# Clustered attention with an expert layer on one core: one-hot rows copied for two head pairs at once, and all five queues in another order

## The chip, the cores and the metric

The kernel runs on one core of a Trainium2 chip. The metric is the device time of one execution in microseconds. The five queues of a core are TensorE (PE), ScalarE (ACT), VectorE (DVE), GpSimd (POOL) and SyncE (SP, which issues DMA transfers).

## The reference

The input is q, k and v of 4 batches, 8 heads, 768 tokens and 64 elements, 16 centroids for each head, and two weight matrices. Each query and key is assigned to the centroid that it is most similar to. A query attends only to keys of its own cluster. The result, as 3072 rows of 512, passes through a layer of two matrix products with h times its softmax and a normalisation between them.

```python
q_assign = argmax(einsum('bhsd,hcd->bhsc', q_n, c_n)); k_assign = ...   # 16 clusters
mask = q_assign[..., :, None] == k_assign[..., None, :]
attn = softmax(where(mask, scale * q @ k.T, -1e9)); x = attn @ v          # (3072, 512)
h = x @ w_in; solu = h * softmax(h)                                       # (3072, 1024)
out = (solu - mean) / sqrt(var + 1e-6) * g_ln @ w_out
```

## The kernel before

**Masking by extra rows.** q and k of a pair of heads (p = 0 to 3 in each batch b) lie in the tiles `qbig` and `kbig`, features on the partitions. Under the 64 features stand one-hot rows of the cluster of each token, so that the product of scores adds a constant where the clusters agree. For batches 1 to 3 the rows 64 to 95 hold 32 rows: the one-hot rows of two heads, one from each of two neighbouring pairs (2d and 2d+1). The same 32 rows are copied into the tile of either pair, and of the odd pair's k the first 16 are set to zero afterwards (`blank`, named `bl`). There are six tiles each of `qbig` and `kbig`, used in turn (`slot`).

**Assignment.** Work comes in pieces: in batch 0 one pair with q and k together, in the other batches q (i = 0) or k (i = 1) of two pairs. A piece is loaded (`ld`, on SP), turned (`xt`, on DVE in batches 1 to 3; on PE with copies `xa` and `xt` in batch 0), cast into `qbig` and `kbig` (`ca`), multiplied with the centroids (`cl`, PE), turned back (`tb`), its maximum taken (`mx`), compared (`oh`), turned again (`ot`), all on DVE, and its one-hot rows are copied into place: `pl`, in `place` on line 458, one copy of 32 rows by 192 words for each pair, half of the tokens and head. v is loaded (`lv`) and cast (`cv`).

**Attention.** A unit n is two tiles of 128 queries of one or two heads. S n.k are its scores in three PSUM banks, E r the exponential of two banks on ACT (144 in all), V n.j the product with v, N g the normalisation of a group of units on DVE. The scores use two PSUM buffers, the exponentials five, the product with v one, so that the V of a group waits for the N of the group before.

**The layer.** For each f of 24 blocks of 128 tokens: `tx` turns x by DMA, `h` is the first product (two halves of two parts, two PSUM buffers), `hm` on DVE moves h out of PSUM with its maximum, `ex` on ACT is the exponential, `u` on DVE or POOL the product, `tu` turns u by DMA, `bn` and `ag` are statistics on DVE, `al` on POOL the factor, `y` the second product (four parts), `sc` on ACT or DVE moves y out of PSUM times the factor, `ou` stores it. `lo`, `li` load the weights, `wi` casts w_in, `su`, `ks`, `me` and `ce` centre w_out.

**The order.** `Plan.ORDER` (lines 23 to 175) lists every operation by name, written out for each of SP, PE, ACT, DVE and POOL. `Plan.run` issues each engine's operations in just that order; an operation may go to any of the engines that `add` allows, and the list it stands in decides. Waits come from the tiles that operations read and write. An engine runs its own list in order, so whatever stands behind a waiting operation waits too.

Of the kernel before, what the change touches and what calls it, by code (L numbers as in the profile page):

```python
# [18 lines left out]
class Plan:  # L19
# [5 lines left out]
            ld0.0.0 ld0.0.1 lg ld0.1.0.0 ld0.1.0 ld0.1.1.0 ld0.1.1 ld0.2.0.0 ld0.2.0  # L25
            ld0.2.1.0 ld0.2.1 lv0.0 ld0.3.0.0 ld0.3.0 ld0.3.1.0 ld0.3.1 lv0.1 lo1 lo0
            lv0.2 lo3 lo2 lv0.3 li0 li2 ld1.0.0.0 li3 li1 ld1.0.0.1 ld1.0.0.2 ld1.0.0
            tx0 ld1.0.1.0 ld1.0.1.1 ld1.0.1.2 ld1.0.1 ld1.1.0.0 ld1.1.0.1 ld1.1.0.2
            ld1.1.0 tx2 ld1.1.1.0 lv1.0 tu0 ld1.1.1.1 ld1.1.1.2 ld1.1.1 lv1.1 ld2.0.0.0
            ld2.0.0.1 ld2.0.0.2 tx4 tu1 ld2.0.0 ld2.0.1.0 tu2 ld2.0.1.1 ou0 ld2.0.1.2  # L30
            ld2.0.1 ld2.1.0.0 ld2.1.0.1 tu3 ld2.1.0.2 ld2.1.0 ou2 ou1 tu4 ld2.1.1.0
            ld2.1.1.1 ld2.1.1.2 ld2.1.1 lv1.2 ou3 ld3.0.0.0 lv1.3 tu5 ld3.0.0.1
            ld3.0.0.2 ld3.0.0 ld3.0.1.0 ld3.0.1.1 ld3.0.1.2 ld3.0.1 lv2.0 tx6 ld3.1.0.0
            ld3.1.0.1 ld3.1.0.2 ld3.1.0 tx8 tx10 lv2.1 ld3.1.1.0 tu6 lv2.2 ld3.1.1.1
            ld3.1.1.2 ou4 ou5 ld3.1.1 tu7 ou6 lv2.3 tu8 lv3.0 ou7 tu9 tu10 ou8 lv3.1
            tu11 lv3.2 ou9 tx12 lv3.3 tx14 ou10 tu12 ou11 tx16 tu13 tu14 ou12 ou13 tu15
# [64 lines left out]
            xa0.0.0 xa0.0.1 xt0.0.1 ca0.0.0.0 ca0.0.0.1 xa0.1.0 xt0.1.0 xa0.1.1 xt0.1.1
            xa0.2.0 xt0.2.0 ca0.1.1.0 xa0.2.1 xt0.2.1 E0 E1 E2 E3 xa0.3.1 E4 xt0.3.1 E5
            E6 E7 E8 E9 E10 E11 E12 E13 E14 ks E15 E16 E17 E18 E19 E20 E21 E22 E23 E24
            E25 E26 ex0 E27 E28 E29 E30 E31 E32 E33 E34 ex1 E35 E36 E37 E38 ex2 E39 sc0
            E40 E41 ca1.2.0 E42 ex3 E43 sc1 E44 ex4 E45 E46 sc2 E47 E48 ca1.2.1 E49 E50
            sc3 E51 ex5 E52 sc4 E53 E54 E55 E56 E57 E58 E59 E60 E61 E62 E63 E64 E65 E66
            sc5 E67 E68 E69 E70 E71 E72 E73 ca2.3.1 E74 E75 ex6 E76 E77 E78 ex7 E79 E80
            E81 E82 E83 ex8 E84 E85 sc6 E86 ex9 E87 sc7 E88 E89 E90 ex10 E91 E92 E93 E94
# [105 lines left out]
def kernel(  # L214
# [57 lines left out]
    def slot(b, p):  # L272
        return (b * n_pair + p) % R
# [784 lines left out]
```

## Time and profile before

| | |
|---|---|
| Median of three runs | 242.8 us (242.77 to 244.27) |
| Profiled execution | 243.15 us, span 241.3 us |
| Mean granted TensorE clock | 0.986 |
| Busy in the span | PE 90%, DVE 81%, ACT 80%, POOL 68% |
| First exponential E0 starts, last E143 ends | 15.57 us, 220.32 us |
| ACT's idle time between exponentials waiting for scores | 23.1 us, longest 4.6 us |
| One-hot copies on POOL, median | 0.34 us |
| One-hot copies on DVE, median and longest | 0.30 us, 1.55 us |

Times in a timeline are counted from the first instruction of the span. An idle time is put down to what ended it. Matmul ends are modelled in the profile, so a busy PE is not PE at its peak.

### The profile page before, as it was taken

The page shows a single profiled execution, that of the slowest core. Times are in us where ns is not written, and L with a number is a line of the kernel's source. Part 1 is how long each engine was busy: PE and PEld are TensorE (multiplying, and loading weights), DVE is VectorE, ACT ScalarE, POOL GpSimd, SP SyncE. Part 2 cuts the span into 40 slices and gives each one's busy share as a digit, 9 for nine tenths or more (in the row PEclk, how much of TensorE's full clock was granted, in tenths as well). Part 3 has the DMA queues.
Part 4 walks back from the last instruction along what each step waited for, and adds up shares of the span by engine and source line. Part 5 has one row for each costly group of instructions (what it writes and reads, how often), then busy time and mean ns, then how long its engine had stood idle before and what let it go on. Part 6 is the DMA issues. An engine that isn't in the chain of part 4 may idle for free.

```text
span 241.3 us, 6307 instructions
## 1 busy us (share of the span) xinstructions
PE 216.2 (90%) x2367; PEld 149.4 (62%) x2400; DVE 195.1 (81%) x432; ACT 193.4 (80%) x238; POOL 163.6 (68%) x275
## 2 busy tenths in 40 slices
PE   1999948798999886999999999999989999998983
PEld 1567625556766553777676767787767687675441
DVE  5399995989798994799799899878999676495992
ACT  2699845877998794999898979899988988897461
POOL 2898990079789987489947889889683512646751
PEclk9999997999999997999999999999999999999999
DMA  7999971899999999997969892857362325447522
GB/s 194 250 274 382 333 174 16 103 180 190 194 160 200 159 224 162 204 186 159 161 132 207 209 222 46 161 148 168 57 147 26 109 46 130 101 80 186 143 87 90
DMA packets 132159, 38.60 MB, mean 160 GB/s; under 512 B 123416, under 2 KB 127520, under 8 KB 132128
## 3 DMA queue, kind: packets, MB, share of 16 engines
q1 hardware_dynamic: 130560, 37.80, 75.3%
q10 hardware_dynamic: 1568, 0.39, 0.7%
q8 instruction: 19, 0.31, 0.6%
q14 instruction: 12, 0.10, 0.1%
HBM read 23.11 MB, written 6.29 MB: 122 GB/s over the span
## 4 chain that ended last, share of the span: by engine, by line
PE 59%; DMA 12%; ACT 10%; DVE 8%; POOL 6%; issue 4%; ACTq 0%; POOLq 0%; DVEq 0%
PE sps L551 18%; PE yps L706 12%; PE hps L638 11%; PE ops L568 10%; DMA xT<-x 8%; ACT e L556 5%; PE csc L428 4%; DMA uT<-u 4%; DVE kbig L408 2%; POOL u L667 2%; ACT xt L381 1%; DVE bs L678 1%; DVE x L591 1%; ACT y L712 1%; PE tp L373 1%
## 5 line engine op out<-in xcount | busy, mean ns | idle before, releaser
L556 ACT ACTIVATE e<-sps 128x1024 bf16<-128x1024 f32 x144 | 141.3, 1023 | 24.4 <-PE sps L551 23.1
L551 PE MATMUL sps<-qbig,kbig 80*128 80x256 bf16 (+4 forms) x648 | 96.4, 265 | 5.8 <-DVE kbig L408 4.3
L551 PEld LDWEIGHTS <-kbig 80*128 80x128 bf16 (+2 forms) x648 | 61.6, 121 | 32.0 <-issue 11.3
L568 PEld LDWEIGHTS <-e 128*128 128x128 bf16 x1152 | 54.4, 98 | 13.8 <-issue 1.6
L568 PE MATMUL ops<-v,e 128*128 128x65 bf16 x1152 | 59.4, 194 | 0.5 <-DVE x L591 0.3
L638 PE MATMUL hps<-w_in_sb,xT 128*128 128x512 bf16 x175 | 50.1, 379 | 4.3 <-DMA xT<-x 2.8
L706 PE MATMUL yps<-w_out_c,uT 128*128 128x512 bf16 x168 | 48.3, 386 | 4.2 <-DMA uT<-u 3.0
L667 POOL TENSOR_TENSOR u<-e_sb,hn 128x1024 bf16<-128x1024 bf16 x16 | 34.3, 2145 | 18.7 <-ACT e_sb L660 18.3
L678 DVE BATCH_NORM_STATS2 bs<-u 128x6 f32<-128x512 bf16 x48 | 32.1, 683 | 0.4 <-POOL u L667 0.2
L660 ACT ACTIVATE e_sb<-hn,hm 128x1024 bf16<-128x1024 f32 (+1 forms) x26 | 28.0, 1078 | 4.5 <-DVE hn L648 4.5
L406 POOL CAST qbig<-xt 64x1536 bf16<-64x1536 f32 (+1 forms) x15 | 19.7, 1312 | 12.5 <-DVE xt L398 11.9
L706 PEld LDWEIGHTS <-uT 128*128 128x128 bf16 x192 | 17.5, 99 | 15.4 <-DMA uT<-u 3.3
L638 PEld LDWEIGHTS <-xT 128*128 128x128 bf16 x192 | 16.8, 97 | 13.1 <-DMA xT<-x 3.3
L648 DVE TENSOR_SCALAR_CACHE_REDUCE hn<-hps 128x512 f32<-128x512 f32 x24 | 16.2, 676 | 8.1 <-PE hps L638 7.3
L458 POOL COPY qbig<-oht 32x192 f32<-32x192 f32 x47 | 18.1, 387 | 6.6 <-DVE oht L448 4.5
L398 DVE STREAM_TRANSPOSE xt<-raw 128x768 f32<-128x768 f32 x24 | 22.2, 951 | 0.2 <-DMA raw<-in_k_dram 0.2
L648 DVE TENSOR_SCALAR_CACHE_REDUCE hn<-hps,hm 128x512 f32<-128x512 f32 x24 | 17.7, 737 | 4.4 <-PE hps L638 4.0
L591 DVE TENSOR_TENSOR x<-ops,den 128x256 bf16<-128x256 f32 (+1 forms) x40 | 19.1, 477 | 1.4
L694 POOL TENSOR_TENSOR esq<-esq,mv 128x1 f32<-128x1 f32 x24 | 5.9, 246 | 20.7 <-DVE mv L682 19.5
L408 POOL TENSOR_SCALAR kbig<-xt 64x1536 bf16<-64x1536 f32 (+1 forms) x14 | 17.6, 1255 | 1.0
L458 POOL COPY kbig<-oht 32x192 f32<-32x192 f32 x46 | 16.3, 356 | 2.2
L696 POOL TENSOR_TENSOR alpha<-esq,halves 128x1 f32<-128x1 f32 x24 | 14.7, 612 | 1.9
(91 smaller groups left out, 220.1 us busy)
## 6 DMA issues: line engine op xcount, KB each, us to landing
vf<-in_v_dram SPq DMA_DIRECT2D x16, 384.0 KB, 4.4
out_dram<-y SPq DMA_DIRECT2D x24, 256.0 KB, 3.1
raw<-in_q_dram SPq DMA_DIRECT2D x31, 192.0 KB, 4.3
raw<-in_k_dram SPq DMA_DIRECT2D x31, 192.0 KB, 4.1
w_g<-in_moe_w_out_dram SPq DMA_DIRECT2D x4, 512.0 KB, 7.1
w_st<-in_moe_w_in_dram SPq DMA_DIRECT2D x4, 512.0 KB, 10.6
uT<-u SPq DMA_TRANSPOSE x22, 3.3
xT<-x SPq DMA_TRANSPOSE x14, 3.6
```

The lines of the kernel that those rows point to most:

```text
L398: nc.vector.transpose(xts[b, d, i][:, hh], raws[b, d, i][:, hh])
L408: eng.tensor_scalar(dst, src, scalar1=inv_C, scalar2=1.0, op0=Alu.mult, op1=Alu.mult)
L458: (nc.vector if e == "DVE" else nc.gpsimd).tensor_copy(dst, src)
L551: nc.tensor.matmul(sps_[r][:, half, c0:c0 + w], kbig[z][u, h % 2, keys], qbig[z][u, h % 2, q0:q0 + w])
L556: nc.scalar.activation(es[r][:], sps_[r][:], Act.Exp, scale=exp_scale, bias=-exp_scale)
L568: nc.tensor.matmul(opss[g][:, s, :VW], es[r][:, half, c0:c0 + P], v1[slot(b, h // 2)][:, h % 2, kt, :VW], start=(kt == 0), stop=(kt == n_t ...
L638: nc.tensor.matmul(ff[f, "h", f2][:], xTs[f // 2][:, f % 2, dc, :], w_in_sb[:, dc, f2 * FF2:(f2 + 1) * FF2], start=(dc == 0), stop=(dc == ...
L648: nc.vector.tensor_scalar(ff[f, "hn"][:, f2, :], ff[f, "h", f2][:], scalar1=-1.0, scalar2=hm[:, 0:1] if f2 else None, op0=Alu.mult, op1=Al ...
L660: nc.scalar.activation(ff[f, "e"][:, r, :], ff[f, "hn"][:, r, :], Act.Exp, scale=-1.0, bias=ff[f, "hm"][:, 1:2], accum_out=ff[f, "esum"][: ...
L667: (nc.vector if e == "DVE" else nc.gpsimd).tensor_tensor(ff[f, "u"][:, r, :], ff[f, "e"][:, r, :], ff[f, "hn"][:, r, :], op=Alu.mult)
L678: nc.vector.bn_stats(ff[f, "bs"][:, f2, :], ff[f, "u"][:, f2, :])
L706: nc.tensor.matmul(ff[f, "y"][:], ff[f, "uT"][:, fc, :], w_out_c[:, fc, :], start=(fc == 0), stop=(fc == n_fc - 1))
```

## The change

The six tiles of q become three tiles that hold two pairs each, and so do those of k; `qbig` and `kbig` are now views of them. In batches 1 to 3 a piece's one-hot rows are copied by four operations `pd` (one for each head and half of the tokens) in place of eight `pl`: each writes the rows into both pairs, reading its source twice. The waits of scores and of `blank` name `pd` accordingly. In batch 0 nothing of this changes. There are 48 operations fewer.

All five lists are written anew. The number of operations on each engine goes from 147, 713, 210, 327 and 207 (SP, PE, ACT, DVE, POOL) to 147, 713, 207, 326 and 163. Of the operations that stay, 24 go from POOL to DVE, 20 from DVE to POOL, 10 from ACT to DVE, 7 from POOL to ACT, 2 from DVE to ACT and 2 from ACT to POOL. 76 `pl` leave POOL and 20 leave DVE; 41 `pd` come to POOL and 7 to DVE.

```diff
     R = 6
-    qbig = [big.tile([P, 2, S], BF16, name=f"qbig{i}") for i in range(R)]
-    kbig = [big.tile([P, 2, S], BF16, name=f"kbig{i}") for i in range(R)]
+    both = [[big.tile([P, 2, 2, S], BF16, name=f"{n}big{i}") for i in range(R // 2)] for n in "qk"]
+    qbig, kbig = ([t[:, pp] for t in ts for pp in range(2)] for ts in both)
...
+    def place_both(b, d, i, c, e):
+
+        hh, hf = divmod(c, 2)
+        (nc.vector if e == "DVE" else nc.gpsimd).tensor_copy(
+            both[i][slot(b, 2 * d) // 2][D:D + NB, :, hh, hf * HALF:(hf + 1) * HALF].bitcast(F32),
+            asg[(b, d, i), "oht"][c * NB:(c + 1) * NB, :].bitcast(F32).unsqueeze(1)
+            .to_broadcast([NB, 2, HALF // 2]))
...
-        return [f"pl{t[0]}.{2 * t[1] + pp}.{t[2]}.{hf}.{hh}" for pp in range(2) for hh in range(2)
-                for hf in range(2)]
+        return [f"pd{tag[j]}.{c}" for c in range(4)]
...
+            if by_token(b):
+                add(nm, "DVE POOL", (lambda e, x=x: place(*x, e)), [f"ot{n}"] + behind(x[0], x[1], "S"))
+            else:
+                add(nm, "DVE POOL", (lambda e, x=x: place_both(*x, e)),
+                    [f"ot{n}"] + behind(b, 2 * x[1], "S") + behind(b, 2 * x[1] + 1, "S"))
...
-            nd += [f"pl{b}.{p}.{t}.{hf}.{hh}" for t in range(2) for hf in range(2)]
+            nd += [f"pl{b}.{p}.{t}.{hf}.{hh}" if by_token(b) else f"pd{b}.{p // 2}.{t}.{2 * hh + hf}"
+                   for t in range(2) for hf in range(2)]
```

Of the lists, the parts that matter here. SP, from the weights on:

```diff
-            lv0.2 lo3 lo2 lv0.3 li0 li2 ld1.0.0.0 li3 li1 ld1.0.0.1 ld1.0.0.2 ld1.0.0
-            tx0 ld1.0.1.0 ld1.0.1.1 ld1.0.1.2 ld1.0.1 ld1.1.0.0 ld1.1.0.1 ld1.1.0.2
...
-            ld2.0.1 ld2.1.0.0 ld2.1.0.1 tu3 ld2.1.0.2 ld2.1.0 ou2 ou1 tu4 ld2.1.1.0
+            lo0 lo1 ld1.0.0.0 ld1.0.0.1 lo2 ld1.0.0.2 ld1.0.0 li2 lv0.3 ld1.0.1.0 li0
+            li3 ld1.0.1.1 ld1.0.1.2 li1 tx0 ld1.0.1 lv1.0 ld1.1.0.0 ld1.1.0.1 tx2
...
+            ld2.0.1.2 tu3 ld2.0.1 ou1 ld2.1.0.0 ld2.1.0.1 ou2 ld2.1.0.2 ld2.1.0 tu4
```

PE, where h0 and y4 stand:

```diff
-            S15.1 S15.2 S16.0 V14.0 V14.1 S16.1 V15.0 V15.1 S16.2 h0.0.0 h0.0.1 h0.1.0
-            S17.0 h0.1.1 S17.1 S17.2 cl1.0.0 h1.0.0 S18.0 S18.1 V16.0 h1.0.1 S18.2 V16.1
...
-            y3.2 y3.3 V31.1 S34.0 S34.1 V32.0 V32.1 y4.0 S34.2 y4.1 S35.0 y4.2 y4.3
+            S15.1 S15.2 S16.0 S16.1 V14.0 V14.1 S16.2 V15.0 S17.0 V15.1 S17.1 S17.2
+            cl1.0.0 S18.0 V16.0 S18.1 V16.1 S18.2 h0.0.0 h0.0.1 S19.0 h0.1.0 h0.1.1
...
+            S33.2 y3.2 y3.3 V31.1 S34.0 S34.1 V32.0 V32.1 S34.2 S35.0 y4.0 y4.1 S35.1
+            S35.2 V33.0 y4.2 S36.0 S36.1 y4.3 V33.1 S36.2 S37.0 V34.0 V34.1 V35.0
```

DVE, its first 50 operations or so:

```diff
-            xt0.0.0 gk tb0.0 mx0.0 oh0.0 ot0.0 pl0.0.1.1.1 pl0.0.1.1.0 pl0.0.0.0.0 bl0.0
-            pl0.0.0.0.1 tb0.1 mx0.1 oh0.1 ot0.1 pl0.1.0.1.0 xa0.3.0 tb0.2 pl0.1.1.0.1
-            xt0.3.0 mx0.2 pl0.1.1.1.1 oh0.2 N0 pl0.1.0.0.1 ot0.2 pl0.2.1.1.1 tb0.3 mx0.3
-            N1 pl0.2.1.0.1 pl0.2.1.1.0 oh0.3 pl0.2.0.1.1 ot0.3 N2 ca0.3.1.0 ca0.3.0.0
-            pl0.3.0.1.0 pl0.3.1.1.0 pl0.3.0.0.0 N3 ca0.3.0.1 ca0.3.1.1 N4 ce0 ce1 ce2 N5
-            ce3 ce4 ce5 N6 ce6 ce7 xt1.0.0.0 xt1.0.0.1 hm0.0 N7 hm0.1 tb1.0.0 mx1.0.0
+            xa0.0.1 xt0.0.0 ca0.0.0.0 gk xa0.1.0 tb0.0 mx0.0 oh0.0 ot0.0 pl0.0.1.1.1
+            tb0.1 pl0.0.1.0.0 mx0.1 pl0.0.0.0.0 bl0.0 ca0.1.0.0 xt0.2.1 oh0.1 ot0.1
+            tb0.2 pl0.1.0.1.0 mx0.2 oh0.2 cv0.0.1 pl0.1.1.0.1 pl0.1.1.1.0 pl0.1.0.0.0
+            xt0.3.0 ot0.2 cv0.1.1 pl0.1.0.1.1 N0 xt0.3.1 pl0.2.1.1.1 ca0.2.0.0
+            pl0.2.0.1.0 N1 tb0.3 mx0.3 pl0.2.0.1.1 oh0.3 ot0.3 N2 pl0.3.1.1.0 cv0.2.0
+            cv0.2.1 pl0.3.0.0.0 N3 pl0.3.0.1.1 pl0.3.1.0.1 ca0.3.0.1 xt1.0.0.0 N4
+            xt1.0.0.1 cv0.3.0 ce0 ce1 N5 ce2 ce3 ce4 N6 ce5 ce6 ce7 N7 wi1 tb1.0.0
+            mx1.0.0 oh1.0.0 ot1.0.0 hm0.0 hm0.1 N8 xt1.0.1.0 xt1.0.1.1 hm1.0 hm1.1 N9
```

POOL, at the end of batch 0:

```diff
-            ca0.2.1.1 cv0.2.0 pl0.3.1.0.0 pl0.3.1.0.1 pl0.3.1.1.1 bl0.3 pl0.3.0.1.1
-            cv0.2.1 pl0.3.0.0.1 wi0 cv0.3.0 cv0.3.1 wi2 wi3 wi1 ca1.0.0 ca1.1.0 u0
+            pl0.2.0.0.1 ca0.3.1.1 ca0.3.1.0 bl0.2 ca0.3.0.0 pl0.3.1.1.1 pl0.3.1.0.0
+            pl0.3.0.0.1 pl0.3.0.1.0 bl0.3 cv0.3.1 ca1.0.0 wi3 wi2 wi0 pd1.0.0.0 ca1.1.0
```

The other rows of the lists differ in the same manner: the operations are the same, save for those that are named above, and stand a few places earlier or later. ACT has E28 before `ex0` in place of E26, and `sc4`, `sc7`, `sc11`, `sc13` and `sc16` have gone from it to DVE, `sc22` has come.

More of the change, by code (lines that the diff above doesn't have):

```diff
@@ L97 @@
-            ptx23 h22.1.1 y19.0 y19.1 y19.2 y19.3 h23.0.0 h23.0.1 h23.1.0 y20.0 y20.1
-            y20.2 y20.3 h23.1.1 ptu22.0 y21.0 y21.1 y21.2 y21.3 ptu22.1 ptu23.0 y22.0
-            y22.1 y22.2 ptu23.1 y22.3 y23.0 y23.1 y23.2 y23.3""",
-        ACT="""
[L101 to L108, printed above, removed]
-            E95 ex11 E96 E97 E98 E99 E100 E101 E102 E103 E104 E105 E106 sc11 E107 E108
-            E109 E110 ex12 E111 E112 E113 ex13 E114 E115 E116 ex14 E117 E118 E119 sc12
-            E120 E121 ex15 E122 sc13 E123 E124 ex16 E125 E126 E127 E128 E129 E130 E131
-            E132 E133 E134 ex17 E135 E136 ex18 E137 E138 sc16 E139 ex19 E140 E141 ex20
-            sc17 E142 E143 ex21 sc18 ex22.0 sc19 ex22.1 sc20 tu22.0 ex23.0 ex23.1 sc21
-            tu23.0 sc23""",
@@ new lines @@
+            V8.1 S11.0 V9.0 V9.1 S11.1 S11.2 me S12.0 S12.1 S12.2 S13.0 V10.0 V10.1
+            V11.0 V11.1 S13.1 S13.2 S14.0 S14.1 V12.0 S14.2 S15.0 V12.1 V13.0 V13.1
+            S15.1 S15.2 S16.0 S16.1 V14.0 V14.1 S16.2 V15.0 S17.0 V15.1 S17.1 S17.2
+            cl1.0.0 S18.0 V16.0 S18.1 V16.1 S18.2 h0.0.0 h0.0.1 S19.0 h0.1.0 h0.1.1
+            V17.0 V17.1 h1.0.0 h1.0.1 S19.1 S19.2 S20.0 h1.1.0 V18.0 h1.1.1 S20.1 V18.1
+            S20.2 S21.0 V19.0 V19.1 S21.1 S21.2 cl1.0.1 S22.0 V20.0 S22.1 h2.0.0 S22.2
@@ new lines @@
+        ACT="""
+            xa0.0.0 xt0.0.1 ca0.0.1.0 xt0.1.0 ca0.0.1.1 xa0.1.1 xt0.1.1 ca0.0.0.1
+            ca0.1.0.1 xa0.2.0 xt0.2.0 xa0.2.1 ca0.1.1.0 E0 E1 E2 E3 xa0.3.0 E4 E5
+            xa0.3.1 E6 E7 E8 E9 ca0.2.1.0 E10 E11 E12 E13 E14 E15 ks E16 E17 E18 E19 E20
+            E21 E22 E23 E24 E25 E26 E27 E28 ex0 E29 E30 E31 E32 ex1 E33 E34 E35 ca1.1.1
+            E36 E37 sc0 ex2 E38 E39 E40 E41 ex3 E42 ca1.3.0 E43 E44 sc1 ex4 E45 E46 sc2
+            E47 ca2.1.0 E48 ca1.2.1 E49 E50 sc3 E51 E52 E53 ex5 E54 E55 E56 E57 E58 E59
+            E60 E61 E62 E63 E64 E65 E66 sc5 E67 E68 E69 E70 E71 E72 E73 E74 E75 E76 ex6
+            E77 E78 E79 E80 ex7 E81 E82 E83 E84 sc6 E85 ex8 E86 E87 ex9 E88 E89 E90 ex10
+            E91 E92 E93 E94 E95 ex11 E96 E97 E98 E99 E100 E101 E102 E103 E104 E105 E106
+            E107 E108 E109 ex12 E110 E111 E112 E113 E114 ex13 E115 E116 ex14 E117 ex15
+            E118 sc12 E119 E120 ex16 E121 E122 E123 E124 E125 E126 E127 E128 E129 E130
+            E131 E132 E133 E134 ex17 E135 E136 E137 ex18 E138 ex19 E139 E140 ex20 E141
+            sc17 E142 E143 ex21 sc18 sc19 ex22.0 ex22.1 sc20 tu22.0 ex23.0 ex23.1 sc21
+            tu23.0 sc22 sc23""",
@@ new lines @@
+        POOL="""
+            z1 z3 cb z5 z2 ca0.1.1.1 pl0.0.0.1.1 pl0.0.1.0.1 pl0.0.0.1.0 pl0.0.1.1.0 sg
+            pl0.0.0.0.1 cv0.0.0 z4 pl0.1.1.1.1 pl0.1.1.0.0 bl0.1 ca0.2.0.1 pl0.1.0.0.1
+            cv0.1.0 pl0.2.1.1.0 pl0.2.1.0.1 ca0.2.1.1 pl0.2.0.0.0 pl0.2.1.0.0
+            pl0.2.0.0.1 ca0.3.1.1 ca0.3.1.0 bl0.2 ca0.3.0.0 pl0.3.1.1.1 pl0.3.1.0.0
+            pl0.3.0.0.1 pl0.3.0.1.0 bl0.3 cv0.3.1 ca1.0.0 wi3 wi2 wi0 pd1.0.0.0 ca1.1.0
+            pd1.0.0.3 u0 pd1.0.0.1 ca1.0.1 pd1.0.0.2 pd1.0.1.0 al0 cv1.0.1 cv1.0.0
+            pd1.0.1.2 u1 pd1.0.1.3 u2 ca1.2.0 bl1.1 u3 al1 al2 cv1.1.0 ca1.3.1 u4
+            ca2.0.0 pd1.1.0.1 pd1.1.0.2 pd1.1.1.1 al3 pd1.1.1.3 cv1.1.1 pd1.1.1.0
+            pd1.1.1.2 al4 pd1.1.0.3 cv1.2.1 pd2.0.0.3 u5 ca2.2.0 ca2.0.1 pd2.0.0.0 bl1.3
+            ca2.1.1 al5 cv1.3.0 pd2.0.0.1 ca2.3.0 pd2.0.1.1 pd2.0.1.2 ca3.0.0 pd2.0.1.0
+            pd2.0.1.3 bl2.1 pd2.1.0.2 ca2.2.1 pd2.1.0.0 pd2.1.0.3 pd2.0.0.2 ca2.3.1
+            pd2.1.1.2 pd2.1.1.1 pd2.1.0.1 u6 pd2.1.1.3 cv2.1.1 pd2.1.1.0 u7 ca3.1.0 al6
+            cv2.2.0 al7 u8 bl2.3 u9 u10 al8 cv2.2.1 pd3.0.1.1 cv2.3.0 cv2.3.1 pd3.0.1.2
+            al9 pd3.0.0.2 pd3.0.1.0 bl3.1 al10 cv3.0.1 pd3.0.0.3 ca3.0.1 al11 pd3.1.0.1
+            cv3.2.0 pd3.1.1.1 cv3.0.0 pd3.1.1.2 u12 pd3.1.0.2 pd3.1.0.0 ca3.2.1 ca3.2.0
+            u13 pd3.1.0.3 al12 cv3.1.1 al13 u16 bl3.3 ca3.3.0 al14 al15 cv3.3.1 u17 al16
+            u18 u19 al17 u20 al18 u21 al19 al20 al21 al22 al23""",
@@ L855 @@
             x = tuple(map(int, nm[2:].split(".")))
-            add(nm, "DVE POOL", (lambda e, x=x: place(*x, e)), [f"ot{n}"] + behind(x[0], x[1], "S"))
+            if by_token(b):
[3 more added lines that the diff above has]
+                    [f"ot{n}"] + behind(b, 2 * x[1], "S") + behind(b, 2 * x[1] + 1, "S"))
     for b, p in pairs:
@@ L862 @@
             add(f"bl{b}.{p}", "DVE POOL", (lambda e, b=b, p=p: blank(b, p, e)),
-                [f"pl{b}.{p}.1.{hf}.{hh}" for hf in range(2) for hh in range(2)])
+                [f"pd{b}.{p // 2}.1.{c}" for c in range(4)])
     def make_c_b2():
```

206 lines of the change are left out of this document (87 added, 119 removed).

## The prediction

> **What bounds the kernel now.** First the page: busy time by engine.
>
> ```profile
> span 241.3 us, 6307 instructions
> PE 216.2 (90%) x2367; PEld 149.4 (62%) x2400; DVE 195.1 (81%) x432; ACT 193.4 (80%) x238; POOL 163.6 (68%) x275
> ```
>
> TensorE (PE) is the nearest to full, ScalarE (ACT) and VectorE (DVE) follow, GpSimd (POOL) has the most room. So the average names no bound; the table by stage does.
>
> ```profile
> 33.00:37.40 4.40, 0.47 (x5) 0.42 (x6) 4.33 (x3) 0.00 (x0) 3.46 (x5) 1.00 0.48 76
> 37.40:42.00 4.60, 4.60 (x41) 2.98 (x39) 2.26 (x5) 3.30 (x4) 0.00 (x0) 0.63 0.00 0
> ```
> ```profile
> 16.00:31.00 15.00, 14.67 (x192) 10.08 (x192) 14.24 (x34) 14.32 (x17) 13.14 (x27) 1.00 1.06 357
> ...
> 70.00:93.00 23.00, 19.30 (x191) 12.35 (x194) 21.65 (x47) 19.05 (x23) 20.90 (x32) 0.98 1.02 183
> 93.00:125.00 32.00, 31.72 (x375) 22.76 (x379) 24.77 (x53) 28.26 (x31) 22.75 (x39) 0.96 0.97 165
> 125.00:141.00 16.00, 15.50 (x174) 10.93 (x174) 14.71 (x33) 14.46 (x19) 13.19 (x19) 1.00 0.91 208
> 141.00:175.00 34.00, 33.43 (x387) 24.96 (x391) 28.99 (x67) 30.80 (x35) 28.50 (x47) 1.00 0.61 130
> ```
>
> The columns are length, then busy time of PE, PEld, DVE, ACT, POOL, then clock and DMA. From 93 to 175 us PE is busy 97 to 99% of the time: there it sets the pace. At 33 to 37.4 us PE and ACT stand still while DVE is busy. The list of waits and the timelines say why.
>
> ```profile
> ACT e L556 <- PE sps L551: 23.1, 29, 4.6
> ```
> ```profile
> 30.86 0.56 DVE L406 CAST qbig<-xt 64x768 bf16<-64x768 f32 x1
> 31.34 5.54 DVE L408 TENSOR_SCALAR kbig<-xt 64x768 bf16<-64x768 f32 x1
> ```
> ```profile
> 31.57 1.03 POOL L492 CAST w_in_sb<-w_st 128x1024 bf16<-128x1024 f32 x1
> 32.56 0.95 POOL L473 CAST v<-vf 128x384 bf16<-128x384 f32 x2
> 33.46 3.00 POOL L492 CAST w_in_sb<-w_st 128x1024 bf16<-128x1024 f32 x3
> ```
>
> The cast `ca0.3.1.1` takes 5.54 us; its like took 0.62 at 27.72. It ends when POOL's run of six casts ends (36.46), and these follow one another without a gap, each starting 0.05 us before its forerunner ends. The scores of head 7 wait for it, and E16 behind them: ACT idle 4.61 us. A second loss lies around 90 us:
>
> ```profile
> 94.93 1.02 ACT L556 ACTIVATE e<-sps 128x1024 bf16<-128x1024 f32 x1 [3.38 <-PE sps L551]
> ```
> ```profile
> 42.62 1.35 SPq L604 DMA_TRANSPOSE xT<-x  x1
> ...
> 87.27 1.29 SPq L672 DMA_TRANSPOSE uT<-u  x1
> ```
>
> S34.2 stands behind y4.0 on PE, which waits for uT of f=4 to land at 92.05. Its u ended at 81.61, but SP issued its turn at 87.27: SP issues back to back from tx0 at 42.62 on, after 7.77 us in which it only waited to issue tx0.
>
> **The change part by part.** *The copies.* 96 copies of 32x192 become 48 of 32x384.
>
> ```profile
> L458 POOL COPY qbig<-oht x47: 333/340/1073, 13.7 to 187.6; 32x192 f32<-32x192 f32 x47
> L458 DVE COPY qbig<-oht x17: 184/300/1553, 13.8 to 178.6; 32x192 f32<-32x192 f32 x17
> ```
>
> Columns: min/median/max ns. On POOL 76 go and 41 come, on DVE 20 go and 7 come. The trace has no 32x384 copy. On POOL its bounds are one old copy (0.34) and two (0.68); the nearest row is the cast of 128x384 to v, 0.50, which I take: 76 x 0.34 = 25.8 becomes 41 x 0.50 = 20.5, so -5.3 us, bounds -11.9 to +2.1. On DVE the bounds are 0.25 and 0.60 (one copy, two); I take 0.35, as v's cast there: 20 x 0.30 = 6.0 becomes 2.5, so -3.5, bounds -4.3 to -1.8. POOL's part is worth nothing in the sum: PE's matmuls cover it from 93 us on; without that cover it would be its 5.3 us.
>
> *Operations that change engine.* POOL to DVE 24, DVE to POOL 20, ACT to DVE 10, POOL or DVE to ACT 9. With the rows' medians and the copies above POOL's whole queue falls from 156 to 148.5 us, DVE's grows from 194 to 197.5, ACT's stays at 188. DVE grows because four more evictions of y (0.75 each), v casts, `wi1` and three early copies come to it.
>
> *The stall at 31 us goes.* `ca0.3.1.1` moves to POOL, ahead of `bl0.2`. DVE keeps one such cast, `ca0.3.0.1`, but POOL's neighbours are then `bl0.3` (0.41) and `cv0.3.1` (0.50); behind these POOL stands at `ca1.0.0`, which waits for `xt1.0.0.1`, two transposes behind the cast on DVE. So the long run of casts can't meet it: -4.6. With PE not idle for 4 us I expect the clock of 0.63 at 37.4 to 42 to rise, and E18's wait of 1.28 behind the mean matmul (1.71) to fall to some 0.8: -0.5.
>
> *DVE's queue in batch 0.* Ahead of N3 sixteen operations come (four copies of x by 0.55, three casts by 0.66, four v casts by 0.35, five one-hot copies) and ten go: 6.5 against 3.2, so +3.3. `xa0.0.1`, `ca0.0.0.0` and `xa0.1.0`, together 1.7, fit into DVE's idle 1.32 and 1.89 before tb0.0 at 10.45. That leaves +1.6; four more operations that can meet POOL, at some 0.15 each, make it +2.2 (bounds 0 and 3.9). Queued behind are N0 to N3, for which V2, V4, V6 and V8 wait.
>
> *h0 and the weights.* SP now issues three loads of piece 1.0.1 (1.55, 0.73, 1.36) before tx0, in the time in which it waited; PE runs S17 and S18 before h0. E25's wait of 2.08 goes. But `wi1` now stands on DVE before tb1.0.0 and hm0 (0.65 by the 64x768 casts of 0.56 to 0.63; at most POOL's 1.03), and h0 comes later, so ex0 will wait for hm0; from E28's place to hm0's I reckon 1.8. Together -0.3, bounds -2.1 to +2.
>
> *y4.* SP's lead is those 3.6 us and what N5, for which tx0 waits, comes earlier. S34.2 and S35.0 pass y4.0. Up to 3.4 is to be had (u of f=4 goes from DVE to POOL, 1.21 to 2.14, which the 5.7 us that its turn stood in SP's queue cover). What is late next is DVE, 94% busy from 70 to 93: between N8 and N14 it gets 2.3 more (two transposes of the next batch, one oh and ot, less u4). So -1.1, bounds -3.4 to +2.3.
>
> *From 97 us on.* I summed the matmuls that stand ahead of each E on PE: the two orders differ by 1.4 us at most. A lead is carried to the end, nothing is added. The four evictions on DVE cost 3.0 there, hidden by PE, since DVE is 77 and 85% busy at 93 to 125 and 141 to 175; without this cover they cost 3.0 and their waits (2.8 us over six rows of L714, so 1.9 over four).
>
> The sum: -4.6 - 0.5 + 2.2 - 0.3 - 1.1 = -4.3 us. The profiled execution took 243.15 (span 241.3), 0.35 above the median of 242.8; 243.15 - 4.3 gives 238.9.
>
> **The rivals.** *The lead is larger.* If DVE's 2.3 us between N8 and N14 are covered and ex0 waits for nothing, the terms are -5.1 + 2.2 - 2.1 - 3.4 = -8.4: 234.8. For it: SP is late with every turn from 65 to 92 us (u3 ended at 77.66, its turn went at 82.54). Against: 94% on DVE.
>
> *The stall moves.* `cv0.3.0` on DVE stands directly behind `xt1.0.0.1`, the operation that also frees POOL's `ca1.0.0`, behind which `wi3 wi2 wi0` are ready. If POOL starts first and runs without a gap, DVE waits 1.46 + 3 x 1.03 less the overlaps = 4.4, and V10, ce0 and N5 with it: 243.3. For it: the six casts at 31 us. Against: DVE starts its next operation some 0.08 before the last ends, POOL began `ca1.0.0` 0.06 after.
> The Trainium skill ("SBUF — State Buffer", "Who interferes with whom") says that whichever of the two issues first holds the shared pair for its whole instruction; read as one instruction, DVE would wait 1.46 us at most and the time would be 240.4 by that estimate. The trace disagrees with that reading: at 31.34 DVE waited through six.
>
> *Hidden anyway.* ACT's chain of exponentials and PE from 93 us on take back all that was won before, say all but 1 us: 242.1. For it: the 97 to 99%. Against: PE's work ahead of each E is unchanged, so there is nothing to take it back.
>
> *Slower: DVE becomes the bound.* If DVE's queue has no usable idle time between N0 and N33, its tally decides: ahead of N33 it has 6.6 us more than before, the stall of 4.9 is off it, and the four evictions wait 1.9: 243.15 + 6.6 - 4.9 + 1.9 = 246.7. It decides from the point where DVE's share passes PE's in the windows from 50 us on. For it: 95% at 16 to 31 and 94% at 70 to 93. Against: 77% after 93.
>
> That the joined copy doesn't do what it says, and costs two old ones, adds 2.1 on POOL, hidden: no other time.
>
> **How the numbers follow.** Forecast 42%, with a range of its own of 236.8 to 240.8; larger lead 12%, stall moved 12%, hidden 10%, slower 24%. About 1% (2.4 us) is what a measurement of this kernel can tell from no change. Faster by more: the larger lead and nearly all of the forecast, 0.52. Within: the stall moved, hidden, and the forecast's upper edge, 0.24. Slower: 0.24. The range goes from 235.0 to 246.5, which cuts the outer halves of the two end cases.
>
> **What would show it.** Right: E16 at 33 to 35 us instead of 37.42, no ACT wait over 2 us before 60, tx0 issued near 39, the turn of f=4 before 83, E54 4 to 5 us before its 97.63, POOL's copies at 0.45 to 0.55. Wrong: a DVE cast of over 2 us beside POOL casts (`cv0.3.0` first of all), N3 after 34, DVE busier than PE from 141 to 175, or a lead at 97 us that is gone at 200.

## The result and the profile after

The changed kernel takes 233.15 us (median of 4 runs, 231.92 to 234.03) against 243.54 of the kernel before beside it: ratio 0.956, 95% interval 0.949 to 0.963, so 10 us less. Run a second time, with four runs more, it took 232.22, ratio 0.959 [0.954, 0.964]. The forecast of 238.9 lies above, and so does the lower end of its range, 235.0. Of the rivals the larger lead, 234.8, came nearest.

The page of the profiled execution (231.92 us):

```profile
span 229.9 us, 6272 instructions
PE 213.6 (93%) x2368; PEld 148.0 (64%) x2400; DVE 189.8 (83%) x431; ACT 193.6 (84%) x235; POOL 152.0 (66%) x231
```

Nearly the same work of PE now fills 93% of a shorter span. The stages (length, PE, PEld, DVE, ACT, POOL, clock, DMA share, GB/s):

```profile
31.00:43.00 12.00, 10.84 (x153) 7.84 (x154) 11.20 (x25) 10.84 (x13) 5.87 (x9) 1.00 0.84 226
70.00:93.00 23.00, 22.59 (x240) 15.08 (x242) 20.37 (x44) 22.72 (x26) 20.46 (x30) 1.00 1.09 200
93.00:125.00 32.00, 31.72 (x393) 23.57 (x398) 28.23 (x61) 28.79 (x33) 26.53 (x34) 1.00 0.88 171
125.00:141.00 16.00, 15.78 (x167) 10.84 (x169) 14.32 (x33) 14.41 (x19) 11.06 (x14) 1.00 0.78 174
141.00:175.00 34.00, 33.10 (x371) 24.79 (x376) 28.08 (x61) 29.80 (x36) 24.64 (x37) 1.00 0.53 127
```

From 70 to 93 us PE was busy 19.30 of 23 us and is now busy 22.59, while DVE fell from 21.65 to 20.37. From 93 us on PE's shares are much what they were. ACT's waits for scores, in all, times, longest:

```profile
ACT e L551 <- PE sps L546: 14.2, 34, 1.1
```

They were 23.1 in all and 4.6 at the longest. The stall of 31 us is gone: on POOL's timeline `ca0.3.1.1` is the first of these two casts (0.83 us each), and on DVE's the cast `cv0.3.0` behind the transpose, where one rival saw the stall move to, takes 0.32.

```profile
26.18 1.73 POOL L398 TENSOR_SCALAR kbig<-xt 64x768 bf16<-64x768 f32 x2
```
```profile
36.23 0.97 DVE L388 STREAM_TRANSPOSE xt<-raw 128x768 f32<-128x768 f32 x1
37.12 0.32 DVE L468 CAST v<-vf 128x384 bf16<-128x384 f32 x1
```

The turn of f=4 goes at 81.11 in place of 87.27, and PE stands 0.24 us ahead of y4.0 where it stood 2.69. SP's queue after:

```profile
36.92 4.25 SPq L484 DMA_DIRECT2D w_st<-in_moe_w_in_dram  x1
41.27 1.66 SPq L599 DMA_TRANSPOSE xT<-x  x1
...
81.11 2.29 SPq L667 DMA_TRANSPOSE uT<-u  x1
```

PE at y4.0, before and after (in brackets the idle time ahead of it and what ended it):

```profile
92.09 0.61 PE L706 MATMUL yps<-w_out_c,uT 128*128 128x512 bf16 x1 [2.69 <-DMA uT<-u]
```
```profile
85.44 1.04 PE L701 MATMUL yps<-w_out_c,uT 128*128 128x512 bf16 x3 [0.24 <-DMA uT<-u]
```

SP issues the load `li1` straight ahead of tx0 at 41.27; the 7.77 us in which it only waited are filled. The joint copies (min/median/max ns):

```profile
L450 POOL COPY qbig<-oht x21: 496/500/722, 48.3 to 169.7; 32x384 f32<-32x384 f32 x21
L450 DVE COPY kbig<-oht x4: 352/368/1442, 57.9 to 166.1; 32x384 f32<-32x384 f32 x4
```

Where the 11.4 us between the two spans were won, by the starts of the same exponentials (ACT's list has `ex0` and `ex5` in other places, so rows beside these are not taken):

| from, to | before | after | won |
|---|---|---|---|
| start to E12 | 27.54 | 30.08 | -2.5 |
| E12 to E20 (the stall) | 15.01 | 9.21 | 5.8 |
| E20 to E51 | 46.86 | 45.71 | 1.2 |
| E51 to E54 (y4) | 8.22 | 4.06 | 4.2 |
| E54 to E143 | 121.67 | 120.53 | 1.1 |
| E143 to the end | 22.00 | 20.31 | 1.7 |

The table is of one execution of either kernel. The experiments show which of its rows hold for others: not all of the 4.2 at y4 does.

### The profile page after: what moved, and what is told of

The parts are those of the page before. It is cut to its first block, busy times and chain, and to the rows that moved or that the text cites. A ratio compares the mean times of both kernels' runs of the same rounds, so it can differ in the third digit from the quotient of the medians.

```text
span 229.9 us, 6272 instructions
## 1 busy us (share of the span) xinstructions
PE 213.6 (93%) x2368; PEld 148.0 (64%) x2400; DVE 189.8 (83%) x431; ACT 193.6 (84%) x235; POOL 152.0 (66%) x231
## 4 chain that ended last, share of the span: by engine, by line
PE 69%; DVE 13%; ACT 7%; issue 4%; POOL 3%; DMA 3%; ACTq 0%; POOLq 0%; DVEq 0%
PE sps L546 21%; PE hps L633 15%; PE yps L701 14%; PE ops L563 12%; ACT e L551 5%; PE csc L418 4%; DMA uT<-u 2%; DVE qbig L445 1%; DVE mx L428 1%; PE tp L363 1%; ACT y L707 1%; DVE oht L438 1%; DVE oh L432 1%; DVE cst L424 1%; DVE xt L373 1%
## 5 line engine op out<-in xcount | busy, mean ns | idle before, releaser
L546 PE MATMUL sps<-qbig,kbig 80*128 80x256 bf16 (+4 forms) x648 | 94.1, 262 | 2.0 <-ACT e L551 1.1
L563 PEld LDWEIGHTS <-e 128*128 128x128 bf16 x1152 | 52.4, 97 | 13.5 <-DVE x L586 1.5
L563 PE MATMUL ops<-v,e 128*128 128x65 bf16 x1152 | 57.2, 193 | 1.1 <-DVE x L586 1.0
L662 POOL TENSOR_TENSOR u<-e_sb,hn 128x1024 bf16<-128x1024 bf16 x19 | 40.7, 2144 | 25.0 <-ACT e_sb L655 19.0
L701 PE MATMUL yps<-w_out_c,uT 128*128 128x512 bf16 x166 | 46.3, 379 | 2.0 <-ACT y L707 0.5
L701 PEld LDWEIGHTS <-uT 128*128 128x128 bf16 x192 | 17.4, 97 | 12.6 <-issue 1.3
L398 POOL TENSOR_SCALAR kbig<-xt 64x1536 bf16<-64x1536 f32 (+1 forms) x12 | 15.2, 1270 | 5.2 <-ACT xt L371 4.3
L396 POOL CAST qbig<-xt 64x1536 bf16<-64x1536 f32 (+1 forms) x12 | 16.3, 1355 | 0.7 <-DVE den L575 0.4
L575 DVE RECIPROCAL den<-ops 128x4 f32<-128x4 f32 (+1 forms) x40 | 7.1, 178 | 10.8 <-PE ops L563 10.7
L450 POOL COPY qbig<-oht 32x384 f32<-32x384 f32 x21 | 10.7, 510 | 6.4 <-DVE oht L438 4.4
L707 ACT ACTIVATE y<-yps,alpha 128x512 f32<-128x512 f32 x13 | 8.9, 686 | 6.8 <-POOL esq L687 2.6
```

Of the source, the lines that this page charges most:

```text
L396: eng.tensor_copy(dst, src)
L546: nc.tensor.matmul(sps_[r][:, half, c0:c0 + w], kbig[z][u, h % 2, keys], qbig[z][u, h % 2, q0:q0 + w])
L563: nc.tensor.matmul(opss[g][:, s, :VW], es[r][:, half, c0:c0 + P], v1[slot(b, h // 2)][:, h % 2, kt, :VW], start=(kt == 0), stop=(kt == n_t ...
L662: (nc.vector if e == "DVE" else nc.gpsimd).tensor_tensor(ff[f, "u"][:, r, :], ff[f, "e"][:, r, :], ff[f, "hn"][:, r, :], op=Alu.mult)
L701: nc.tensor.matmul(ff[f, "y"][:], ff[f, "uT"][:, fc, :], w_out_c[:, fc, :], start=(fc == 0), stop=(fc == n_fc - 1))
```

## The experiments

Ratios are to runs of the kernel before beside them on the same chip, with the 95% interval; 0.01 is 2.4 us. Profiled executions are single ones: one can lie 2 us or more beside its kernel's median, which is said where it matters.

**The order alone: `after_single`.** All lists of the changed kernel, with the old tiles and each joint copy written as its two old ones.

```diff
-    ... pd1.0.0.0 ca1.1.0 pd1.0.0.3 u0 ...
+    ... pl1.0.0.0.0 pl1.1.0.0.0 ca1.1.0 pl1.0.0.1.1 pl1.1.0.1.1 u0 ...
```

> The new lists with the old copies: each joint copy is replaced by the two single copies, one behind the other on the same engine, and the tiles are those of before. Theory 1, the order of the lists brings the gain and the joint copies next to nothing: 233 to 235 us, POOL some 7 us busier (41 x 0.17), E52 within 1 us of its 85.90. Theory 2, the joint copies bring it because they free GpSimd and VectorE in the stretch from 60 to 93 us: 238 us or more, u of f=4 and N14 late by 2 us or more, and the lead at E52 back to some 4.

237.70 us, 0.982 [0.974, 0.990]. The order without the joint copies has less than half of the gain. (Its profiled execution, 239.61, is the longest of its four.)

**The copies alone: `before_joint`.** The old lists with joint copies, each in the place where the earlier of its two stood.

> The old lists with the joint copies: each stands where the earlier of its two single copies ran, nothing else moves. Theory 1 (order): 242 to 243.5 us, the 5.5 us cast at 31 us and E52's wait of 3.4 are still there. Theory 2 (copies): 236 to 239 us, E52's wait gone.

240.34 us, 0.994 [0.991, 0.997]: 1.5 us. Here the copies are worth little, there they were worth 5.

**The stall alone: `before_cast_pool`.** One name moves:

```diff
-  DVE:  ... N3 ca0.3.0.1 ca0.3.1.1 N4 ...
+  DVE:  ... N3 ca0.3.0.1 N4 ...
-  POOL: ... pl0.3.0.0.1 wi0 cv0.3.0 ...
+  POOL: ... pl0.3.0.0.1 ca0.3.1.1 wi0 cv0.3.0 ...
```

> The old lists with one operation moved: ca0.3.1.1 goes from VectorE to GpSimd, just ahead of wi0. Theory 1: the cast takes 0.8 us there, E16 starts near 33 instead of 37.4, and 3 to 4 us of lead at E20 stay to the end: 239 to 240 us. Rival: tx0, the loads behind it and y4 keep their places, so the lead is lost by E28 or at E52: 242 to 243 us.

235.51 us, 0.975 [0.969, 0.980]: 6.2 us from one cast, which is more than the stall. POOL's timeline:

```profile
32.17 0.83 POOL L419 TENSOR_SCALAR kbig<-xt 64x768 bf16<-64x768 f32 x1
33.06 1.04 POOL L503 CAST w_in_sb<-w_st 128x1024 bf16<-128x1024 f32 x1
34.04 0.96 POOL L484 CAST v<-vf 128x384 bf16<-128x384 f32 x2
34.94 3.01 POOL L503 CAST w_in_sb<-w_st 128x1024 bf16<-128x1024 f32 x3
```

The cast takes 0.83, POOL's six still follow, and nothing of DVE meets them. E12 to E20 takes 9.33 us in place of 15.01. That is 5.7: some 4.4 of wait by E16, and 1.3 behind it, with the clock at 1.00 where it was 0.63 at 37.4 to 42. Of the stage with the stall the profile before is not the longest: in `before_joint` and `before_y4`, which keep it, E12 to E20 takes 16.06 and 15.97 us. So 6.2 for the median is no contradiction.

**y4's place alone: `before_y4`.** The old lists, S34.2 and S35.0 ahead of y4.0 on PE.

```diff
-  ... V32.1 y4.0 S34.2 y4.1 S35.0 y4.2 ...
+  ... V32.1 S34.2 S35.0 y4.0 y4.1 y4.2 ...
```

> The old lists with S34.2 and S35.0 ahead of y4.0 on TensorE, nothing else. If y4's wait for the turn of f=4 cost the exponentials its 3.4 us, and this place alone decides: E52 starts near 91.5, E53 waits instead by 2 us at most, 239.5 to 241 us. Rival, the prediction's: what is late next (the turn of f=4 itself, issued at 87.3, or VectorE) takes it over, E53 waits the same 3 us, 242 to 243 us.

242.64 us, 1.008 [1.003, 1.012]: no gain, by the interval even a small loss.

**y4's transpose alone: `before_tu4`.**

```diff
-  SP: ... tu3 ld2.1.0.2 ld2.1.0 ou2 ou1 tu4 ld2.1.1.0 ...
+  SP: ... tu3 tu4 ld2.1.0.2 ld2.1.0 ou2 ou1 ld2.1.1.0 ...
```

> The old lists, only the transpose tu4 moved ahead in SP's queue, directly behind tu3, past ld2.1.0.2, ld2.1.0, ou2 and ou1. u4 is done at 81.6 us, so tu4 would be issued near 83.8 instead of 87.3. Theory 1 (SP's queue sets y4.0): the wait of PE ahead of y4.0, 2.7 us in the profile before, is gone, E52 comes 2.5 to 3.3 us earlier, and 1.5 to 3 us of it reach the end: 239 to 240.5. Theory 2 (DVE, 94 % busy in this stretch, is late next): E52 1 us earlier at most, the end within 1 us of the kernel before.

242.62 us, 0.999 [0.994, 1.003]. In its profiled execution (240.13, the lowest of ten) PE doesn't wait for uT there at all; the median is that of the kernel before. The old kernel's runs on one chip spread over 238.5 to 243.2, and its profiled execution, 243.15, is one with a large loss at y4: with SP's list the same, PE waited 1.3 us at y4.0 in `before_joint` and 0.7 in `before_cast_pool`, not 2.69.

The stretch from E48 to E60, which holds all of y4, says how large. It takes 20.41 us in the profile before, but 17.38 in `before_cast_pool`, 17.42 in `before_joint`, 17.41 in `before_y4`, 17.46 in `before_tu4` and 18.03 in `cast_joint` below (one exception, `cast_joint_lv`, is told there). So some 3 of the 4.2 us in the table are of that one execution. And neither y4's place nor its transpose, moved alone, shortens the stretch. In `before_tu4` something else is late next: POOL waits 2.3 us for the load lv1.2, which SP issues at 92.11, and PE 1.2 us for the cast behind that load. The changed kernel takes 14.99 and 14.72 us in its two profiles; some profiles of kernels with its lists take 16.5 to 17.0, as is told below.

**Two pieces together: `cast_joint`.** The old lists with `before_cast_pool` and `before_joint`; beside it the changed kernel again.

> The old lists with two pieces of the change: ca0.3.1.1 on POOL just ahead of wi0, and the joint copies. Theory 1 (the stall and the copies are the change, and the order of the rest only follows): the two add, 235.5 less 1.4 us, so 233.5 to 234.5, within 1 us of the changed kernel, and a wait of ACT at the place of y4.0 under 0.5 us. Theory 2 (the new order of the queues is worth several us by itself, and the copies help only where POOL has more to do, as it has in the new lists): 235 to 236, no better than the moved cast alone, and the changed kernel stays 2 to 4 us ahead.

> The changed kernel itself once more, as the yardstick for the kernels run beside it: 231 to 234 us, ratio to the kernel before 0.95 to 0.963. Both theories agree on it.

235.21 us, 0.970 [0.965, 0.976], against 232.22, 0.959. So the moved cast brings 6.2 us, the joint copies 1.0 on top, which the intervals can't tell from nothing, and the new lists 2.7 more. Theory 2 has the nearer numbers.

**Where do the copies cost 5 us in the new lists?** In the changed kernel's own tiles, `place_both` makes two copies in place of one, on POOL only, on DVE only, or on both:

```diff
-        eng.tensor_copy(dst, one.unsqueeze(1).to_broadcast([NB, 2, HALF // 2]))
+        for pp in range(2):
+            eng.tensor_copy(dst[:, pp], one)
```

> The new lists with the joint tiles, but each of the 41 joint copies on POOL done as two copies of 32x192, one behind the other; the 7 on DVE stay joint. POOL has 41 times (2 x 0.34 - 0.51) = 7 us more to do. Theory 1 (POOL's queue passes its delay on: u4 and with it the transpose tu4, the alphas, the casts): 2 to 4 us slower than the changed kernel, E52 1.5 to 2.5 us later, the wait of PE ahead of y4.0 about 1 us. Theory 2 (what the single copies cost is the wait of DVE's copies for POOL, not POOL's time): within 1 us of the changed kernel. The prediction, which put the copies at nothing, says the same as theory 2.

> The new lists with the joint tiles, but each of the 7 joint copies on DVE done as two copies of 32x192; the 41 on POOL stay joint. DVE has 7 times (2 x 0.25 - 0.35) = 1 us more to do. Theory 1 (POOL's time is what the single copies cost): within 0.7 us of the changed kernel. Theory 2 (each copy on DVE can be held until POOL pauses, and twice as many are held twice as often): one copy of pd3.1.1.3 takes 3 to 4 us beside the cast and the product on POOL near 167 us, and the kernel is 2 to 5 us slower than the changed one.

> The new lists and the joint tiles, but all 48 joint copies of batches 1 to 3 done as two copies each, one behind the other. Theory 1 (the single copies cost what POOL and DVE need for them, and a later queue of SP at y4.0): the two halves add, 1.1 and 0.9 us, so 234 to 234.5 us, ratio 0.966 to 0.97. Theory 2 (what kernel after_single lost, over 4 us against the changed one, is the old tiles of one pair each, or a chance wait of one DVE copy through two operations on POOL near 170 us): if it is the tiles, 233 to 234.5 here too; if it is the long wait, it is seen here as well, one DVE copy of 3 to 4 us, and the kernel takes 236 to 238.

On POOL 233.28 us, 0.964 [0.958, 0.970]; on DVE 233.15, 0.962 [0.956, 0.967]; on both 237.18, 0.979 [0.973, 0.985]. By the ratios the halves cost 1.2 and 0.7 us, which these runs can't tell from nothing, and both together 4.9, nearly as in `after_single`: so it isn't the tiles, and not the sum of the copies' times. With both split, one place stands out. DVE:

```profile
167.10 3.80 DVE L454 COPY kbig<-oht 32x192 f32<-32x192 f32 x2
```

POOL beside it:

```profile
165.71 1.46 POOL L398 TENSOR_SCALAR kbig<-xt 64x1536 bf16<-64x1536 f32 x1
167.12 1.55 POOL L396 CAST qbig<-xt 64x1536 bf16<-64x1536 f32 x1
168.65 2.13 POOL L663 TENSOR_TENSOR u<-e_sb,hn 128x1024 bf16<-128x1024 bf16 x1
```

These are the two halves of `pd3.1.1.3`. The first starts just ahead of POOL's cast (167.10 against 167.12) and takes 0.25. The second starts at 167.28 and ends at 170.89: it sits out the cast, and the product u13 follows the cast without a gap. The eviction of h behind it is late, PE runs dry,

```profile
171.74 0.59 PE L634 MATMUL hps<-w_in_sb,xT 128*128 128x512 bf16 x2 [2.50 <-DVE hn L644]
```

and its clock falls. The stage of 165 to 180 us, with both split and in the changed kernel run beside the halves:

```profile
165.00:180.00 15.00, 12.22 (x108) 8.28 (x109) 12.25 (x21) 10.41 (x15) 9.98 (x14) 0.89 0.51 114
```
```profile
165.00:180.00 15.00, 14.69 (x150) 10.14 (x151) 13.19 (x27) 13.40 (x19) 10.03 (x12) 1.00 0.57 135
```

`after_single`, with the old tiles, shows the same 3.80 us at 169.65. From E115 to E117, around this place, `after_two_all` takes 7.02 us and `after_single` 7.44, the changed kernel 3.61. If this is the cost, one copy out of 48 left joint must give it back:

> As after_two_all (every joint copy done as two), but the one joint copy pd3.1.1.3, on DVE near 167 us, is left joint. Theory 1 (what the joint copies are worth in the new lists is one event: as two copies this one is held on DVE through the cast and the product u13 on POOL, 3.8 us, and PE runs dry behind it): the event is gone, 232.5 to 234 us, E117 within 3.5 us of E115. Theory 2 (47 more copies in the queues are worth several us together): 235.5 to 237, as with all 48 split.

233.57 us, 0.967 [0.961, 0.972]. E115 to E117 is back at 3.30. So this copy is worth some 3 us (0.979 to 0.967) and the other 47 some 2; the intervals leave either about 2 us of play. As one operation it comes through ahead of the cast, which starts at 167.61:

```profile
167.59 0.35 DVE L454 COPY kbig<-oht 32x384 f32<-32x384 f32 x1
```

In the changed kernel it is met too, by the cast alone, and takes 1.44; u13 starts 0.11 us after the cast has ended there, and the copy gets in. POOL and DVE in its second profile:

```profile
165.97 1.46 POOL L396 CAST qbig<-xt 64x1536 bf16<-64x1536 f32 x1
167.53 2.15 POOL L662 TENSOR_TENSOR u<-e_sb,hn 128x1024 bf16<-128x1024 bf16 x1
```
```profile
166.20 1.44 DVE L450 COPY kbig<-oht 32x384 f32<-32x384 f32 x1
```

Moving that copy to POOL, ahead of u13:

> The changed kernel with one joint copy, pd3.1.1.3, moved from DVE (1.44 us there, waiting beside a cast on POOL) to POOL ahead of u13 (0.51 us). Theory 1 (a wait of DVE for POOL of some 1 us here is on the path): hm14.1 and E117 0.7 to 1 us earlier, 231 to 231.5. Theory 2 (u13, moved 0.5 us later, takes it back): within 0.5 us of the changed kernel.

232.07 us, 0.957 [0.952, 0.963], no difference from the changed kernel that these runs can tell. Its profiled execution, 233.91, shows a difference in the middle of the kernel that no edit made. SP's queue in it and, second, in the changed kernel's:

```profile
62.88 1.29 SPq L610 DMA_TRANSPOSE xT<-x  x1
64.22 0.58 SPq L391 DMA_DIRECT2D raw<-in_q_dram  x1
64.90 3.10 SPq L678 DMA_TRANSPOSE uT<-u  x1
```
```profile
62.33 1.24 SPq L599 DMA_TRANSPOSE xT<-x  x1
63.61 1.53 SPq L380 DMA_DIRECT2D raw<-in_q_dram  x1
65.24 1.47 SPq L667 DMA_TRANSPOSE uT<-u  x1
```

Up to there the lists are the same. tu1 occupies SP for 3.10 us in place of 1.47, and E54 starts at 91.66 in place of 89.06. The eight profiles with the new lists fall into two groups: with tu1 at 1.45 to 1.47 us, E48 to E54 takes 8.6 to 8.9 us (the changed kernel twice, `after_two_all`, `after_two_but_one`); with 2.29 to 3.79 it takes 10.4 to 10.9 (`after_single`, `after_two_pool`, `after_two_dve`, `after_pd_pool`). Joint and single copies are in both, so this lag is no part of what the copies cost.

**A load ahead of its time: `cast_joint_lv`.** `cast_joint` with lv1.2 behind lv1.1 on SP, as in the new lists.

> As cast_joint (old lists, ca0.3.1.1 on POOL, joint copies), with the load lv1.2 moved ahead in SP's queue, from behind ld2.1.1 to behind lv1.1, where the new lists have it. In cast_joint POOL waits 2 us for this load near 91 us and PE 1 us for the cast behind it. Theory 1 (a part of what the new order brings is SP's queue with loads ahead of their time): 233.5 to 234.5, E52 to E60 1 to 2 us shorter. Theory 2 (SP is back to back there, so an earlier load only makes the transposes later): within 0.7 us of cast_joint, 235.

235.48 us, 0.973 [0.966, 0.979], as without. E54 to E60 is 1.1 us shorter (6.86 against 7.96), but tu4 goes at 82.35 in place of 80.76, PE waits 2.8 us for it and E51 to E54 is 3.1 longer in that execution. On this queue, which SP issues nearly back to back, the load brought forward wins nothing; the trace suggests that the transposes behind it pay for it.

**The head of the old lists: `merged` and `merged_sp`.** The changed kernel paid 2.5 us ahead of E12. Both take the old lists, with the cast on POOL, up to `me` on PE, E16 on ACT, N3 and `ca0.3.0.1` on DVE, and the new lists behind. `merged` takes SP's old list up to tx0 and POOL's up to `wi0`; `merged_sp` takes SP's new list and POOL's old one up to `ca0.3.1.1`.

> The changed kernel with the head of the old lists: up to me on PE, E16 on ACT, N3 and ca0.3.0.1 on DVE, wi0 on POOL and tx0 on SP as in the old lists with ca0.3.1.1 on POOL, everything behind as in the new lists. Theory 1 (the 2.2 us that the prediction put on the new queue ahead of N3 are real and were paid): E16 near 33.6, the lead of 1.8 us carried to the end, 230 to 231 us. Theory 2 (SP, back to back from 13 to 100 us, sets the stages from 40 us on): the lead at E16 is gone by E54, 231.5 to 234.

> As merged, but with SP's queue of the changed kernel from the start and the old head of the other queues: up to me on PE, E16 on ACT, N3 and ca0.3.0.1 on DVE, ca0.3.1.1 on POOL. In merged DVE waited 4.3 us at xt1.0.0.0 for a load that the old order of SP brings later, with cv0.3.0 behind it. Theory 1 (that mix was the fault, the head of the old lists is 2 us shorter): E16 33 to 34, no ACT wait over 1 us before 45, 230 to 231 us. Theory 2 (what is behind in the new lists is timed to its own head and SP sets it): the lead at E16 is gone by E54, 232 to 234.

`merged`: 237.78 us, 0.981 [0.974, 0.987]. DVE's waits from 33 to 46 us:

```profile
DVE xt L399 <- issue: 4.3, 1, 4.3
```

The view names no cause, but the last load for `xt1.0.0.0`, early in the new list of DVE, lands at 35.59, and it starts at 35.76: the old list of SP brings that load late, and `cv0.3.0` stands behind. `merged_sp`: 233.28, 0.965 [0.960, 0.969]. E16 starts at 33.59, 2.1 us ahead of the changed kernel's 35.65, E24 1.1 ahead, E36 0.3, E48 0.15. DVE's waits from 30 to 50 us say who takes it:

```profile
DVE v L479 <- DMA vf<-in_v_dram: 1.9, 1, 1.9
DVE w_in_sb L498 <- DMA w_st<-in_moe_w_in_dram: 1.1, 1, 1.1
```

They wait for loads in SP's queue. A faster head of the new lists won nothing here, and none of these kernels beats the changed one.

## Why the prediction was wrong, point by point

Foretold were -4.3 us against the profiled execution; it fell by 11.2. Of the views that it named, the turn of f=4 at 81.11 (before 83), POOL's copies at 0.50 and no wait of ACT over 0.7 us from 30 to 60 came as foretold, and N3 at 32.62, within its bound. E16 came at 35.35, just past the 33 to 35. tx0 came at 41.27 (39.71 in the second profile), not near 39. E54 came 8.6 us earlier, not 4 to 5: there it failed.

- **The stall, -4.6 and -0.5 for the clock.** The mechanism was right, the size a little small: 5.8 in the table, 5.7 with the cast moved alone. The median of runs gave 6.2 for it, 1.1 more than the two terms.
- **The stall moves, and DVE as the bound.** Neither came. `cv0.3.0` takes 0.32, and DVE is less busy than PE in every stage from 70 us on.
- **DVE's queue ahead of N3, +2.2.** Its size was right: N3 comes 2.4 us later, and at E36 the changed kernel is still 1.9 us behind `before_cast_pool` (60.19 against 58.28). But DVE isn't alone in it. `merged_sp` took 2.1 us of the delay away, and all but 0.3 was gone by E36, with waits for loads in SP's new queue. The prediction had asked who waits for N3, and not what else those would wait for.
- **y4, -1.1.** This step failed: 4.2 in the trace. Some 3 of it the old kernel's profiled execution, from which the forecast was counted, had by itself. Against the 17.4 us that the other kernels with the old queues mostly take from E48 to E60, the changed kernel's 14.7 to 15.0 are still 2.4 to 2.7, over twice the term. The argument was that DVE, 94% busy from 70 to 93 us, is late next. But a busy share is no lateness: from E48 to E60 of the changed kernel (the line below the list) DVE is 94% busy as well, and PE is 98% busy. Which of the new places brings these 2.4 to 2.7 us stays open: y4's place, its transpose and the load lv1.2, each moved alone, gave nothing.
- **The copies, 0.** This step failed as well. Their durations were right (0.50 and 0.35), and on the old lists 0 was not far off: they are worth 1.5 us alone, and 1.0 on top of the moved cast. In the new lists they are worth 5. They were priced by POOL's time, hidden by PE from 93 us on, and by DVE's time unhindered. The costly thing is a DVE copy held by POOL: 3.61 us for one copy of 0.25, and DVE's list has evictions for PE behind it, so that the cover itself, PE, stood for 2.50 us at 171.74.
- **From 97 us on, 0.** Nearly right for the kernel as it is, with joint copies: 1.1 us to E143. The tail, which no step looked at, gave 1.7 in the table, and 0.8 to 1.5 against the other kernels with the old lists; why isn't shown.

```profile
80.20:95.20 15.00, 14.70 (x182) 10.28 (x185) 14.04 (x28) 14.65 (x18) 13.11 (x22) 1.00 1.09 196
```

So the mechanism of the first term was right, and its size 1.1 us short. The other misses were the tail and the two terms at which the sum put a rival's doubt (DVE's share) or a cover (PE) in place of a look at the next queue.

The new lists with single copies came out at 0.979 and 0.982 of the kernel before, and the forecast was 0.983 of its 243.15 us. Had the copies stayed single, the number would have been right, but by luck: terms that were too small, and a held copy that nobody had foreseen, would nearly have cancelled.

The Trainium skill ("SBUF — State Buffer", "Who interferes with whom") says that when VectorE works in one of its two-port modes, whichever of it and GpSimd issues first holds the shared port pair for its whole instruction. Read as one instruction, the held copy would have waited 1.55 us at most by POOL's rows; the trace shows 3.61, through two instructions that follow one another without a gap. In the changed kernel 0.11 us lies between these two, and the copy got in.

## What to carry to other kernels

An operation on DVE that must wait for POOL can wait for a gap on POOL, not only for the running instruction (here 5.54 us through six casts, and 3.61 through a cast and a product): look at what follows on POOL, and put such an operation where POOL waits for something itself, or make two of them one, as the change does. Where a queue issues back to back, as SP nearly does here from 13 to 100 us, follow its lateness from stage to stage: it can swallow what is gained elsewhere. A stage's busy share names a suspect, not the wait. And a single profile can hold a loss that other executions don't have: compare the same stretch in the profiles of kernels that leave it as it was.

## What the runs showed of the hardware

Two small copies of 0.25 us, one behind the other, cost PE 2.50 us and, with the clock at 0.89 in that stage, the kernel some 3 us, while each half of the same edit, by itself, cost 1.2 and 0.7 us, not to be told from nothing. In these traces it hung on small times whether a copy was held: the first of the two came 0.02 us ahead of POOL's cast and the second behind it, and in the changed kernel, where 0.11 us lies on POOL behind the cast, the copy got in.

The time for which one transpose occupies SP's queue differs from execution to execution with the same list ahead of it: 1.47 and 3.10 us for tu1. With the longer one E54 comes some 2 us later, in four profiles of eight. Whether the transpose itself is the cause, or something that delays both, isn't shown.
